# Batch 0 of a sparse attention: masks as bias matmuls, zero products on TensorE, and the output weights queued part by part

## The chip, the cores and the metric

The kernel runs on one NeuronCore of a Trainium2 chip. Its time is the device time of one execution in microseconds (us), the median of several runs. A NeuronCore has five engines with an instruction queue each: TensorE (PE, matrix products; its weight loads are listed as PEld), VectorE (DVE), ScalarE (ACT), GpSimd (POOL) and SyncE (SP, which here issues only DMAs). They meet through semaphores. SBUF is the on-chip memory with 128 partitions; PSUM takes what TensorE produces. DMAs are issued from the queues of SP, ACT or POOL; those of POOL can change the type on the way (float32 to bfloat16).

## What is computed

The reference is an attention over 8 batches of 8 heads, 576 positions and 64 channels, followed by a two-layer network over the 4608 tokens. Heads 0 to 3 look back over a window of 32 positions (local), heads 4 to 7 at every 32nd earlier position (strided):

```
scores = scale * np.matmul(q, k.transpose(0, 1, 3, 2))
mask_local = (rel >= 0) & (rel < stride)
mask_strided = (rel >= 0) & (pos[None, :] % stride == pos[:, None] % stride)
...
attn = attn / (np.sum(attn, axis=-1, keepdims=True) + 1e-09)
x = np.matmul(attn, v)        # heads joined: 4608 x 512
h = x @ w_in                  # 512 x 2048
g = h * np.tanh(softplus(h))
out = g @ w_out               # 2048 x 512
```

The masks set scores outside the pattern to -1e9 ahead of the softmax.

## The kernel before

**Attention of one batch.** Only the blocks that a mask leaves over are computed. The strided heads are cut into 16 units of 72 x 72 (`S_UNITS`), the local ones into 12 units of 128 keys x 96 queries for two heads (`L_UNITS`); `PARTS` groups them into three parts each, ("s", 0..2) and ("l", 0..2). For a part, `qk` makes the scores in a PSUM tile of the tag `acc0`, `acc1` or `acc2`, and ACT takes their exponential into `P_s` or `P_l` (SBUF, bfloat16). `mask` then multiplies that on an engine by a 0/1 pattern from the constants (L289). `pv` (one block, result in a PSUM tile of the two-buffer tag `pt`) or `pv2` (two blocks, result in an `acc` tile) multiplies by v, which carries a column of ones, so that the row sum comes along; DVE takes the reciprocal and scales into `x_s` or `x_l` (L316 and L317, in `pv2` L330 and L331). `xt` transposes these on PE, and a copy puts them into `xT`, the input of the network: strided rows into chunks 2 and 3, local ones into chunks 0 and 1.

**Transposed q and k.** `qk` needs channels on partitions. For batches 0 and 1, PE transposes them (`t_step`, for the local heads of batch 0 `t_step_loc0`) into a `pt` tile and a copy brings them to `kTs`, `qTs`, `kTl`, `qTl`. From batch 2 on, SP issues DMA transposes (`transpose_str`, `transpose_loc`). Local q and k arrive in float32 in `kl32` and `ql32` (`load_qk_loc`, SP) and are cast into `kl`, `ql`; strided ones are cast by POOL's DMA into `ks`, `qs` (`load_qk_str`). Those of batch 0 come into staging tiles, `st0` (strided, SP) and `lq0` (local, POOL).

**The network.** Block t of 512 tokens goes through `mlp1` (eight groups of eight 128x512 matmuls, L428, each evicted by ACT with the activation) and `mlp2` (64 matmuls, L467). Nine blocks cover the eight batches. In `mlp1(0, ...)` the first two groups are split into halves: chunks 2, 3 of both, then chunks 0, 1 of both.

**Order.** The program is written under a manual schedule: every engine executes its instructions in the order in which the Python code emits them. First comes the head, the attention of batch 0. Then, for each t, `mlp1(t)` runs, and the 16 steps of `mlp2(t)` are interleaved with the attention of batch t + 1 by the lists `at[0]` to `at[15]`. In stage t = 0 all batch-1 transposes of q and k are emitted after the last groups of `mlp1` (pairs `ts[4..5]`, `ts[6..7]`, `ts[0..1]`) and after the first step of `mlp2` (`ts[2..3]`). `mlp2(0)` goes through the chunks of `w_out` in the outer loop: step 0 to 3 need its first part, 4 to 7 the second, 8 to 11 the third, 12 to 15 the fourth.

**The queue of weights.** POOL issues the five loads of `w_in`, those of `ks`, `qs` of batch 1 and the first two parts of `w_out` in this order. A small copy into the tile `held` makes POOL wait: ahead of `w_in` it reads `vs[0]`, so it waits for the DVE cast of batch 0's strided v; in `rest_of_w_out` it reads a corner of `kTl`, and the last two parts of `w_out` and strided q, k of batch 2 follow. On SP a tiny load into `gate` reads the last quarter of `w_in`, so SP waits for its landing ahead of v of batch 1.

Of the kernel before, what the change touches and what calls it, by code (L numbers as in the profile page):

```python
# [10 lines left out]
F32 = mybir.dt.float32  # L11
# [8 lines left out]
SU = 80  # L20
CS, PN = 8, 72
RING = 4


def _consts():

    kk = np.arange(128)[:, None]
    qq = np.arange(WQ)[None, :]
    rel = qq + 32 - kk
    p = np.arange(PN)  # L30
    c = np.zeros((128, 128 + WQ + PN), np.float32)
    c[:, 0:128] = np.eye(128)
    c[:, 128:128 + WQ] = (rel >= 0) & (rel < STRIDE)
    c[:PN, 128 + WQ:] = (p[:, None] % 4 == p[None, :] % 4) & (p[:, None] <= p[None, :])
    return c.astype(ml_dtypes.bfloat16)
# [3 lines left out]
def kernel(ctx, tc, q, k, v, moe_w_in, moe_w_out, out):  # L39
# [14 lines left out]
    xT = const.tile([128, 4, RT], BF16, name="xT")  # L54
    consts = const.tile([128, 128 + WQ + PN], BF16, name="consts_sb")
    ident = consts[:, 0:128]
    loc = consts[:, 128:128 + WQ]
    stm = consts[0:PN, 128 + WQ:128 + WQ + PN]
    vl32 = const.tile([128, 4, NW, D], F32, name="vl32")
    vs32 = const.tile([128, 4, CS, D], F32, name="vs32")  # L60
# [14 lines left out]
    gate = const.tile([1, 256], BF16, name="gate")  # L75
    held = const.tile([1, 4], BF16, name="held")
    x_l = const.tile([128, NW, 256], BF16, name="x_l")
# [9 lines left out]
    def acc(i, name):  # L87

        return ps_a.tile([128, 2, 512], F32, tag=f"acc{i}", name=name)
# [11 lines left out]
    def load_qk_loc(b):  # L101
        for dst, src in ((kl32, k), (ql32, q)):
            if b < 2:
                nc.sync.dma_start(
                    dst[0:PL].rearrange("p h j d -> p h (j d)"),
                    src[b, 0:4].rearrange("h (p j) d -> p h (j d)", j=CL),
                )
            else:
                nc.sync.dma_start(
                    dst[0:PL].rearrange("p h i d -> p (h i) d"),  # L110
                    src[b, 0:4].rearrange("h (i p) d -> p (h i) d", p=PL),
                )
# [27 lines left out]
    def load_w_out(c0, c1):  # L140
        for c in range(c0, c1):
# [3 lines left out]
            )  # L145

    def cast(eng, out_, in_):
        if eng is nc.scalar:
            nc.scalar.copy(out_, in_)  # L149
        else:  # L150
            eng.tensor_copy(out_, in_)  # L151

    def cast_qk_loc(b, e_k, e_q):
        for e, dst, src in ((e_k, kl, kl32), (e_q, ql, ql32)):
            if b < 2:
                cast(e, dst[b % 2][0:PL].rearrange("p j h d -> p h j d"), src[0:PL])
            else:
                to = by_tile(dst[b % 2])
                for hp in range(2):
                    cast(  # L160
                        e, to[:, hp].rearrange("p i e d -> p e i d"), src[0:PL, 2 * hp:2 * hp + 2]
                    )
# [26 lines left out]
    def cast_v_loc(b, eng, i0=0, i1=NW):  # L189
        for i in range(i0, i1, 3):  # L190
            cast(
                eng, vl[b % 2][:, i:i + 3, :, 0:D],
                vl32[:, :, i:i + 3, :].rearrange("p h w d -> p w h d"),
            )
        if i0 == 0:
            eng.memset(vl[b % 2][0:32, 0, :, 0:D], 0.0)
# [34 lines left out]
    def t_step_loc0(src, dst, hp, eng):  # L231

        tr = tile_t("tr")[:].bitcast(BF16)
        for j in range(CL):
            for e in range(2):
                nc.tensor.transpose(
                    tr[64 * e:64 * e + 64, PL * j:PL * j + PL], src[0:PL, 2 * hp + e, j, :],
                    ident[0:PL, 0:PL],
                )
        cast(  # L240
            eng, dst.rearrange("c (p j) -> c p j", j=CL),
            tr[:, 0:S].rearrange("c (j p) -> c p j", j=CL),
        )

    T_ORDER = [(kd, w, hp) for kd in ("s", "l") for hp in range(2) for w in ("k", "q")]
# [13 lines left out]
    class Attn:  # L259
        def __init__(self, b):  # L260
            self.b = b

        def qk(self, parts, i_acc):

            ps, o = acc(i_acc, "ps"), 0
            todo = []
            for kind, i in parts:
                w = WQ if kind == "l" else PN
                o0 = o
                for x, y in PARTS[kind][i]:  # L270
                    for e in range(2):
                        r = slice(64 * e, 64 * e + 64)
                        if kind == "l":
                            lhsT, rhs = kTl[r, y, WQ * x:WQ * x + 128], qTl[r, y, WQ * x:WQ * x + WQ]
                        else:
                            c0 = SU * (4 * y + x)
                            lhsT, rhs = kTs[r, c0:c0 + 128], qTs[r, c0:c0 + PN]
                        nc.tensor.matmul(ps[:, e, o:o + w], lhsT=lhsT, rhs=rhs, start=True, stop=True)  # L278
                    o += w
                todo.append((kind, i, o0, o - o0))  # L280
# [54 lines left out]

        def xt(self, kind, hf, eng=None):
            eng = eng or nc.scalar
            tr = tile_t("trx")[:].bitcast(BF16)
            t0 = (self.b % RING) * S
# [144 lines left out]
    with tc.manual_schedule():  # L484
        Po, Dv, Sc = nc.gpsimd, nc.vector, nc.scalar
        Sc.preload_act_table(AF.Exp)
        Sc.dma_start(consts[:], consts_h.ap())
# [12 lines left out]
        lq0 = g_pool.tile([128, 16, 512], BF16, tag="gT", name="lq0")  # L500
        lq0 = lq0[:].rearrange("p a b -> p (a b)")[0:PL]
        kl0, ql0 = [lq0[:, 1536 * i:1536 * i + 1536].rearrange("p (h x) -> p h x", h=4) for i in range(2)]
        for p in P_l:
            Po.memset(p[:], 0.0)
        for dst, src in ((kl0, k), (ql0, q)):
            Po.dma_start(dst, src[0, 0:4].rearrange("h (p j) d -> p h (j d)", j=CL))
        kl0, ql0 = [x.rearrange("p h (j d) -> p h j d", d=D) for x in (kl0, ql0)]
# [10 lines left out]

        a = Attn(0)
        for hp in range(2):  # L520
            h = 2 * hp
            cast(Dv, ks[0][0:PN, h:h + 2, :], st0[0][:, h:h + 2, :])
            t_step(0, "s", "k", hp, Sc)
        for hp in range(2):
            h = 2 * hp
            cast(Dv, qs[0][0:PN, h:h + 2, :], st0[1][:, h:h + 2, :])
            t_step(0, "s", "q", hp, Dv if hp else Sc)
        for i in range(3):
            a.qk([("s", i)], i)
        a.mask("s", 0, Dv)  # L530
        cast(Dv, vs[0][0:PN, :, :, 0:D], vs32[0:PN])
        a.mask("s", 1, Dv)
        for x in (ks, qs):
            Po.memset(x[1][64:SU], 0.0)
        Po.tensor_copy(held[:], vs[0][0:1, 3, 0, 0:4])
        load_w_in(0, 256)
        load_w_in(256, 512)
        load_w_in(512, 1024)
        cast_v_loc(0, Po, 0, 3)
        load_w_in(1024, 1536)  # L540
        load_w_in(1536, 2048)
        for hp in range(2):
            t_step_loc0(kl0, kTl[:, hp, 32:32 + S], hp, Sc)
        a.pv2("s", 0, 0)
        a.mask("s", 2, Dv)
        a.pv2("s", 2, 1)
        for hp in range(2):
            t_step_loc0(ql0, qTl[:, hp, :], hp, Sc)
        a.qk([("l", 0)], 2)
        a.pv2("s", 4, 0)  # L550
        a.qk([("l", 1)], 1)
        a.mask("l", 0, Dv)
        a.pv2("s", 6, 0)
        cast_v_loc(0, Sc, 3, 6)
        a.qk([("l", 2)], 2)
        a.mask("l", 1, Dv)
        load_qk_str(1)
# [3 lines left out]
        accs = (2, 1, 0)  # L561
        gT, g1 = mlp1(0, accs)
        a.xt("s", 0)
        a.xt("s", 1)
        Sc.preload_act_table(AF.Mish)
        a.pv2("l", 0, 1)
        a.mask("l", 2, Dv)
        a.pv2("l", 2, 0)
        a.pv("l", 4)
        a.pv("l", 5)  # L570
        a.xt("l", 0)
        a.xt("l", 1)
        cast_qk_loc(1, Po, Po)
        for x in (ks, qs):
            Po.memset(x[0][64:SU], 0.0)
        load_qk_loc(2)

        def rest_of_w_out():
            Po.tensor_copy(held[:], kTl[0:1, 1, 32:36])
            load_w_out(2, 4)  # L580
            load_qk_str(2)
            cast_qk_loc(2, Po, Po)

# [4 lines left out]
        for t in range(NBLK):  # L588
# [4 lines left out]
            if t == 0:  # L593
                ts, at = t_steps(1), attn_steps(1, y, y)
                at[0] = [ts[2], ts[3], cast_v1]
                at[6].append(lambda: cast_v_loc(1, Dv, 0, 3))
                at[7].append(lambda: cast_v_loc(1, Dv, 3, 6))
                at[9] += [lambda: transpose_str(2), lambda: load_v_loc(2), lambda: cast_v(2, Po, Po)]
# [7 lines left out]
            for i, g in enumerate(g1):  # L606
                g()
                if t == 0:
                    for n in {7: (4, 5), 8: (6, 7), 9: (0, 1)}.get(i, ()):
                        ts[n]()  # L610
                    if i == 8:
                        rest_of_w_out()
                elif i == 0 and t + 1 < B:
                    if t > 1:
                        cast_qk_loc(t + 1, Dv, Dv)
                    transpose_loc(t + 1)
                    if t + 2 < B:
# [43 lines left out]
```

The softmax here doesn't subtract the row's maximum and nothing guards it: scores larger than these inputs give would overflow.

## Time and profile before

| what | us |
|---|---|
| median of 5 runs (lowest, highest) | 322.27 (320.83, 323.84) |
| the profiled execution's own time | 324.03 |
| its span | 322.2 |
| PE busy (share of the span) | 298.6 (93%) |
| ACT, DVE, POOL busy | 172.6, 131.1, 40.7 |
| head: start to the first matmul of `mlp1(0)` | 0 to 30.07 |
| `mlp1(0)` to the first matmul of `mlp2(0)` | 30.07 to 47.50 |
| `mlp2(0)` with batch 1 | 47.50 to 68.49 |
| stage t = 1 | 68.49 to 101.14 |
| stage t = 2, stage t = 3 | 32.49 each |

A group or an instruction of a view is given as start, duration, engine, line, operation, what it writes and reads, and how often; "idle before" and its releaser tell how long the engine stood still and what let it go. The chain of waits is followed back from the last instruction. The page's row of granted clocks shows 9 in every slice; a slow start of PE has to be read from the spacing of its instructions.

### The profile page before, as it was taken

What the parts mean: (1) busy time and instruction counts of PE and PEld (TensorE: products, weight loads), DVE (VectorE), ACT (ScalarE), POOL (GpSimd) and SP (SyncE); (2) the same over time, 40 slices, a digit from 0 to 9 for tenths busy, and PEclk for the clock granted to TensorE, in tenths of its full rate; (3) what the DMA queues carried; (4) which work ended last, traced back from release to release, by engine and by line L of the source; (5) the groups of instructions that cost most, each with busy time, mean ns of one, the idle gap of its engine ahead of it and who ended that gap; (6) DMA issues with size and microseconds to landing.
All of it is one profiled execution on the core that took longest, in us unless ns stands there. A gap on an engine that the chain in (4) does not pass through costs nothing.

```text
span 322.2 us, 5827 instructions
## 1 busy us (share of the span) xinstructions
PE 298.6 (93%) x2448; PEld 159.6 (50%) x2488; DVE 131.1 (41%) x332; ACT 172.6 (54%) x195; POOL 40.7 (13%) x50
## 2 busy tenths in 40 slices
PE   0674999899999999999999999999999999999996
PEld 0552455454455445544568555445544554444444
DVE  7676046920286128802880288018811830000000
ACT  2581454385646664666466646674567456315601
POOL 9287023045000100000020000000000000000000
PEclk9999999999999999999999999999999999999999
DMA  6999999999999999999979995897650101011012
GB/s 181 217 229 205 229 179 187 172 195 224 150 185 193 178 170 187 258 130 187 224 115 195 185 212 97 173 181 155 86 124 0 67 5 62 0 65 65 2 54 76
DMA packets 103114, 46.72 MB, mean 145 GB/s; under 512 B 85168, under 2 KB 95728, under 8 KB 103088
## 3 DMA queue, kind: packets, MB, share of 16 engines
q1 hardware_dynamic: 91648, 37.22, 64.1%
q0 software_dynamic: 11152, 8.92, 19.3%
q8 instruction: 19, 0.31, 0.4%
q10 hardware_dynamic: 288, 0.21, 0.2%
q14 instruction: 7, 0.06, 0.1%
HBM read 38.34 MB, written 9.44 MB: 148 GB/s over the span
## 4 chain that ended last, share of the span: by engine, by line
PE 83%; DVE 12%; issue 2%; DMA 1%; ACT 1%; ACTq 0%
PE psh L428 39%; PE pso L467 28%; PE po L305 4%; PE pso L449 4%; PE ps L278 3%; DVE x_l L317 3%; DVE Pl L289 2%; DVE x_s L317 2%; PE trx L344 2%; DVE ks L151 1%; DVE rden L316 1%; DMA st<-in_k_dram 1%; PE trx L354 1%; PE tr L207 1%; DVE vl L151 1%
## 5 line engine op out<-in xcount | busy, mean ns | idle before, releaser
L428 PE MATMUL psh<-xT,w_in 128*128 128x512 bf16 (+1 forms) x628 | 127.8, 362 | 0.8 <-issue 0.2
L467 PE MATMUL pso<-w_out,gT 128*128 128x512 bf16 x485 | 121.5, 379 | 1.7 <-issue 0.6
L433 ACT ACTIVATE gT<-psh 128x1024 bf16<-128x1024 f32 x72 | 73.6, 1023 | 45.5 <-PE psh L428 44.2
L428 PEld LDWEIGHTS <-w_in 128*128 128x128 bf16 x640 | 63.1, 99 | 63.3 <-issue 3.3
L467 PEld LDWEIGHTS <-gT 128*128 128x128 bf16 x512 | 43.6, 97 | 39.0
L289 DVE TENSOR_TENSOR Ps<-Ps,consts_sb 72x864 bf16<-72x864 bf16 (+1 forms) x24 | 13.2, 551 | 88.3 <-ACT Ps L283 88.3
L149 ACT COPY xT<-trx 128x576 bf16<-128x576 bf16 x32 | 20.1, 639 | 40.9 <-PE trx L354 28.2
L474 ACT COPY osb<-pso 128x1024 f32<-128x1024 f32 x16 | 16.2, 1012 | 22.6 <-PE pso L467 13.8
L283 ACT ACTIVATE Ps<-ps 72x864 bf16<-72x864 f32 (+1 forms) x24 | 18.5, 803 | 13.3 <-PE ps L278 13.2
L316 DVE RECIPROCAL rden<-po 72x4 f32<-72x4 f32 (+1 forms) x100 | 17.4, 174 | 17.2 <-PE po L305 17.1
L317 DVE TENSOR_TENSOR x_s<-po,rden 72x256 bf16<-72x256 f32 x56 | 23.6, 421 | 1.9
L151 DVE COPY osb<-pso 128x512 f32<-128x512 f32 (+1 forms) x2 | 1.1, 558 | 54.5 <-PE pso L449 54.5
L283 ACT ACTIVATE Pl<-ps 128x960 bf16<-128x960 f32 (+1 forms) x24 | 18.7, 806 | 3.6 <-PE ps L278 3.5
L305 PEld LDWEIGHTS <-Ps 72*128 72x128 bf16 x256 | 13.9, 101 | 12.9 <-DVE Ps L289 2.3
L317 DVE TENSOR_TENSOR x_l<-po,rden 96x256 bf16<-96x256 f32 x44 | 18.5, 421 | 1.5
L305 PE MATMUL po<-vs,Ps 72*128 72x65 bf16 x256 | 17.6, 201 | 1.4 <-DVE vs L151 0.8
L305 PE MATMUL po<-vl,Pl 128*128 128x65 bf16 x192 | 12.9, 201 | 5.4 <-DVE Pl L289 3.8
L289 DVE TENSOR_TENSOR Pl<-Pl,consts_sb 128x960 bf16<-128x960 bf16 (+1 forms) x24 | 16.2, 677 | 0.0
L97 POOL DMA_DIRECT2D ks<-in_k_dram x7 | 5.3, 762 | 81.9 <-DMA kTs<-ks 81.9
L305 PEld LDWEIGHTS <-Pl 128*128 128x128 bf16 x192 | 9.9, 103 | 9.6 <-DVE Pl L289 4.0
L449 PE MATMUL pso<-w_out,gT 128*128 128x512 bf16 (+1 forms) x79 | 14.0, 336 | 0.1
L151 DVE CAST vl<-vl 128x768 bf16<-128x768 f32 x12 | 10.9, 943 | 1.3 <-DMA vl<-in_v_dram 1.3
(70 smaller groups left out, 177.6 us busy)
## 6 DMA issues: line engine op xcount, KB each, us to landing
out_dram<-osb SPq DMA_DIRECT2D x16, 512.0 KB, 3.8
vl<-in_v_dram SPq DMA_DIRECT2D x7, 768.0 KB
vs<-in_v_dram SPq DMA_DIRECT2D x8, 576.0 KB
kl<-in_k_dram SPq DMA_DIRECT2D x7, 576.0 KB, 7.6
ql<-in_q_dram SPq DMA_DIRECT2D x7, 576.0 KB, 10.5
w_out<-in_moe_w_out_dram POOLq DMA_DIRECT2D x4, 512.0 KB, 15.9
ks<-in_k_dram POOLq DMA_DIRECT2D x7, 288.0 KB, 8.0
qs<-in_q_dram POOLq DMA_DIRECT2D x7, 288.0 KB, 9.3
```

The source lines that it names most:

```text
L149: nc.scalar.copy(out_, in_)
L151: eng.tensor_copy(out_, in_)
L283: nc.scalar.activation(pt[0:n, :, 0:nw], ps[0:n, :, o0:o0 + nw], AF.Exp, scale=scale)
L289: meng.tensor_tensor(out=pm, in0=pm, in1=mk[0:n, :].unsqueeze(1).unsqueeze(1).to_broadcast([n, 2, nu, w]), op=ALU.mult,)
L305: nc.tensor.matmul(po[:, h, :], lhsT=pt[0:n, c0:c0 + 128], rhs=rhs, start=True, stop=True,)
L316: nc.vector.reciprocal(rden[0:m, :], po[0:m, :, D])
L317: nc.vector.tensor_tensor(out=dst.rearrange("p (h d) -> p h d", h=4), in0=po[0:m, :, 0:D], in1=rden[0:m, :].unsqueeze(2).to_broadcast([m, ...
L428: nc.tensor.matmul(ps[:, u, o:o + n], lhsT=w_in[:, cc, fc * 128:(fc + 1) * 128], rhs=xT[:, cc, a:a + n], start=(cc == 2), stop=(cc == 1),)
L433: nc.scalar.activation(gT[:, 2 * g:2 * g + 2, :], ps[:], AF.Mish)
L449: nc.tensor.matmul(p, lhsT=gT[:, fc, 128 * ot:128 * ot + 128], rhs=w_out[:, fc, c0:c1], start=(fc == 0), stop=(fc == 15),)
L467: nc.tensor.matmul(p[:, ot % 2, :], lhsT=gT[:, fc, 128 * ot:128 * ot + 128], rhs=w_out[:, fc, :], start=(fc == 0), stop=(fc == 15),)
L474: nc.scalar.copy(osb[:], p[:])
```

## The change

In the head, batch 0 is no longer masked by DVE. `bias` writes the mask pattern, -30000 where a score is to vanish, into PSUM by two matmuls with the identity, and `qk` adds the scores to it. `busy` and the argument `n_busy` of `xt` emit products of a zeroed tile. `lq0` moves to partitions 64 to 127 in rows of 9 positions. `clear` zeroes as float32. The strided v cast stands later in DVE's order; `pv2` calls are in part replaced by `pv`; local v of batch 0 is cast in three pieces by POOL, ACT and DVE; the order of the local parts in `pv2` changes.

The wait ahead of `w_in` is now for `ql0`. The third part of `w_out` is queued after the first transposes into `kTs` of batch 1 (`rest_of_w_out`, after the tenth step of `mlp1(0)`), the fourth after the first mask of batch 1 (`last_of_w_out`, step 2 of `mlp2(0)`), followed by q, k of batch 2 and the casts of local v of batch 1, which DVE did before, and of local q, k of batch 2. In stage t = 1 PE transposes local q and k of batch 2, after groups 5 and 6 of `mlp1(1)`; SP's four DMA transposes of that batch go away, and its loads have the rows of 6 positions that batches 0 and 1 have.

```diff
@@ constants, loads and casts @@
+C0, P0 = 9, 64
...
+    c[:, o:o + WQ] = -30000.0 * (1 - c[:, 128:128 + WQ])
+    c[:PN, o + WQ:] = -30000.0 * (1 - c[:PN, 128 + WQ:o])
...
+    zero = const.tile([128, 128], BF16, name="zero")
...
-            if b < 2:
+            if b < 3:
...
+    def clear(eng, x):
+        eng.memset(x.bitcast(F32), 0.0)
...
+    def busy(n, i_acc):
+        ps = acc(i_acc, "ps")
+        for _ in range(n):
+            nc.tensor.matmul(ps[:, 0, 0:128], lhsT=zero[:], rhs=zero[:], start=True, stop=True)
...
+        def bias(self, kind, i, i_acc):
+            n, w, mk = (128, WQ, locb) if kind == "l" else (PN, PN, stmb)
+            nu = len(PARTS[kind][i])
+            ps = acc(i_acc, "ps")
+            for e in range(2):
+                nc.tensor.matmul(
+                    ps[:, e, 0:nu * w].rearrange("p (u c) -> p u c", u=nu), lhsT=ident[0:n, :],
+                    rhs=mk.unsqueeze(1).to_broadcast([n, nu, w]), start=True, stop=True,
+                )
+            return ps
...
-                        nc.tensor.matmul(ps[:, e, o:o + w], lhsT=lhsT, rhs=rhs, start=True, stop=True)
+                            ps[:, e, o:o + w], lhsT=lhsT, rhs=rhs, start=first, stop=True,
...
@@ the head @@
         for p in P_l:
-            Po.memset(p[:], 0.0)
+            clear(Po, p[:].rearrange("p e c -> p (e c)"))
...
+        busy(40, 0)
         for hp in range(2):
...
             t_step(0, "s", "k", hp, Sc)
+            if hp == 0:
+                busy(8, 0)
+        sb = [a.bias("s", i, i) for i in (1, 2)]
+        busy(8, 0)
+        sb.insert(0, a.bias("s", 0, 0))
...
-            a.qk([("s", i)], i)
-        a.mask("s", 0, Dv)
-        cast(Dv, vs[0][0:PN, :, :, 0:D], vs32[0:PN])
-        a.mask("s", 1, Dv)
+            a.qk([("s", i)], i, sb[i])
+        Po.tensor_copy(held[P0:P0 + 1], ql0[0:1, 3, 0, 0:4])
+        load_w_in(0, 256)
         for x in (ks, qs):
-            Po.memset(x[1][64:SU], 0.0)
-        Po.tensor_copy(held[:], vs[0][0:1, 3, 0, 0:4])
-        load_w_in(0, 256)
+            clear(Po, x[1][64:SU].rearrange("p h x -> p (h x)"))
...
-        cast_v_loc(0, Po, 0, 3)
+        cast_v_loc(0, Po, 0, 2)
...
-            t_step_loc0(kl0, kTl[:, hp, 32:32 + S], hp, Sc)
-        a.pv2("s", 0, 0)
-        a.mask("s", 2, Dv)
-        a.pv2("s", 2, 1)
+            t_step_loc0(kl0, kTl[:, hp, 32:32 + S], hp, Sc if hp else Dv)
+        cast(Dv, vs[0][0:PN, :, :, 0:D], vs32[0:PN])
+        lb = [a.bias("l", i, i) for i in range(2)]
         for hp in range(2):
             t_step_loc0(ql0, qTl[:, hp, :], hp, Sc)
-        a.qk([("l", 0)], 2)
-        a.pv2("s", 4, 0)
-        a.qk([("l", 1)], 1)
-        a.mask("l", 0, Dv)
-        a.pv2("s", 6, 0)
-        cast_v_loc(0, Sc, 3, 6)
-        a.qk([("l", 2)], 2)
-        a.mask("l", 1, Dv)
+        a.pv2("s", 0, 2)
+        a.qk([("l", 0)], 0, lb[0])
+        a.qk([("l", 1)], 1, lb[1])
+        a.pv("s", 2)
+        a.pv("s", 3)
+        a.pv2("s", 4, 2)
+        a.qk([("l", 2)], 0, a.bias("l", 2, 0))
+        a.pv("s", 6)
+        a.pv("s", 7)
+        cast_v_loc(0, Sc, 2, 4)
+        cast_v_loc(0, Dv, 4, 6)
+        a.pv2("l", 2, 1)
...
+        a.pv2("l", 0, 2)
         a.xt("s", 0)
         a.xt("s", 1)
         Sc.preload_act_table(AF.Mish)
-        a.pv2("l", 0, 1)
-        a.mask("l", 2, Dv)
-        a.pv2("l", 2, 0)
-        a.pv("l", 4)
-        a.pv("l", 5)
-        a.xt("l", 0)
-        a.xt("l", 1)
+        a.pv2("l", 4, 0)
+        a.xt("l", 0, n_busy=4)
+        a.xt("l", 1, Dv, n_busy=4)
...
@@ stages t = 0 and t = 1 @@
         def rest_of_w_out():
-            Po.tensor_copy(held[:], kTl[0:1, 1, 32:36])
-            load_w_out(2, 4)
+            Po.tensor_copy(held[0:1], kTs[0:1, 0:4])
+            load_w_out(2, 3)
+
+        def last_of_w_out():
+            Po.tensor_copy(held[0:1], P_s[0][0:1, 0, 0:4])
+            load_w_out(3, 4)
             load_qk_str(2)
+            cast_v_loc(1, Po)
             cast_qk_loc(2, Po, Po)
...
-                at[6].append(lambda: cast_v_loc(1, Dv, 0, 3))
-                at[7].append(lambda: cast_v_loc(1, Dv, 3, 6))
+                at[0].append(lambda: Sc.preload_act_table(AF.Exp))
+                at[2].append(last_of_w_out)
...
-                    if i == 8:
+                    if i == 9:
                         rest_of_w_out()
+                elif t == 1 and i in (5, 6):
+                    for w in ("k", "q"):
+                        t_step(2, "l", w, i - 5)
                 elif i == 0 and t + 1 < B:
                     if t > 1:
                         cast_qk_loc(t + 1, Dv, Dv)
-                    transpose_loc(t + 1)
+                        transpose_loc(t + 1)
```

## The prediction

> **What bounds the kernel now.** I read the sums first, then the chain of waits, then the stages of the chain by time. PE is busy for 93% of the span, and stages t = 2 and 3 take 32.49 us each with 32.00 of PE: nothing to gain there. The head is different, so I read its part of the chain:
>
> ```profile
> 4.64 4.47 DVE ks L151 x2
> ...
> 11.73 0.44 PE ps L278 x8
> 12.19 0.89 ACT Ps L283
> 13.11 0.60 DVE Ps L289
> 13.71 1.15 DVE vs L151
> ...
> 23.08 0.69 DVE x_l L331
> 23.76 3.43 DVE Pl L289
> 27.20 0.13 DVE rden L330
> ...
> 28.64 1.21 PE trx L344 x12
> ```
>
> Two pieces are far too long: two casts of k in 4.47 us, and the smallest mask in 3.43. The timeline of DVE and POOL shows what stood beside them:
>
> ```profile
> 4.46 1.80 POOL L534 MEMSET ks<- 16x2048 bf16 x1
> 4.64 4.46 DVE L151 CAST ks<-st 72x1024 bf16<-72x1024 f32 x2 [0.95 <-DMA st<-in_k_dram]
> 6.20 2.35 POOL L534 MEMSET qs<- 16x2048 bf16 x1
> 9.02 1.27 DVE L151 CAST qs<-st 72x1024 bf16<-72x1024 f32 x2
> ...
> 23.68 3.51 DVE L289 TENSOR_TENSOR Pl<-Pl,consts_sb 128x384 bf16<-128x384 bf16 x1
> 24.09 1.48 POOL L151 CAST kl<-kl 96x1536 bf16<-96x1536 f32 x1
> 25.51 1.47 POOL L151 CAST ql<-ql 96x1536 bf16<-96x1536 f32 x1
> ```
>
> The same two casts of q take 1.27 without POOL; the same mask form took 0.35 in batch 1 (57.08). So the excesses are 3.2 and 3.1 us. Next, weight loads at the start of `mlp1(0)`:
>
> ```profile
> 34.34 0.15 PEld L428 LDWEIGHTS <-w_in 128*128 128x128 bf16 x1 [0.28 <-issue]
> 34.73 1.18 PEld L428 LDWEIGHTS <-w_in 128*128 128x128 bf16 x6 [0.24 <-issue]
> ```
>
> From 30.07 to 34.73 they are 0.427 us apart; later the chain gives 9.93/46 = 0.216 a matmul. Eleven intervals at the difference are 2.3 us of slow PE. Last, the table of stretches:
>
> ```profile
> 47.50:68.49 20.99, 19.58 (x222) 10.96 (x223) 15.32 (x42) 10.13 (x13) 4.55 (x7) 1.00 1.23 174
> 82.31:101.14 18.83, 18.50 (x202) 9.90 (x205) 12.35 (x38) 10.29 (x13) 0.00 (x0) 1.00 1.35 172
> ```
>
> Columns: length, then busy PE, PEld, DVE, ACT, POOL. `mlp2(0)` leaves PE idle for 1.4 us, against 0.3 one block later; the chain passes through DVE there, by the two casts of vl at 57.43 and 59.16.
>
> [...]
>
> **Head, rebuilt from its rows.** POOL's clears of P_l, 2.25 before, should halve with half the elements (bounds 1.1 to 2.25), and so lq is issued about 1.1 us earlier. POOL then waits for ql0, and nothing of it stands beside the k casts. What limits instead is the landing of q: its second half landed at 8.5 by the trace's semaphore updates; I take 9.0, as lq now competes earlier (bounds 8.5 to 10). Then:
> - cast 0.67, transposes 0.6, DVE copy 0.46, scores 0.5: 11.3, against 12.19.
> - ACT: three exponentials 0.89 + 0.89 + 0.65, then the second k copy 0.64, which frees the transpose buffer: 14.4. The transposes of q stand next on PE and ahead of the first PV (0.65 + 0.5): 15.6. The strided v cast (1.22) must be done by then; POOL's two clears (about 0.9 each) can stand beside it, and cost 0 to 1 us. I take 0.
> - DVE: two pairs at 0.20 + 0.69, four singles at 0.17 + 0.42 take 4.2: 19.8; the vl cast of a third (two thirds of 0.94) 0.6: 20.4; three local pairs 2.7: 23.1. The masks of batch 0 (3.3 us without the excess) are gone; PE gains six bias pairs, 432 columns at most, 0.36 a matmul at half clock, and they fall into waits for q and for ACT.
> - last transposes 0.6 and issue 0.22: `mlp1(0)` starts at 23.9 instead of 30.07.
>
> [...] The groups of 8 and 4 cost 0.9 and 0.4 at most, behind casts and x_l scaling. Bounds of what they save: 0 to 2.3 us of slow PE.
>
> **`mlp1(0)`.** Before, 30.07 to 47.47 is 17.4: 13.8 (as in block 1) + 2.3 slow + three transpose pairs. Warm, 15.2 remain: 23.9 + 15.2 = 39.1; slow, 41.4.
>
> **The weights have to be there.** The first part of w_out, issued at 21.77, landed 20.7 us later, at 42.5, because five w_in loads and ks, qs stand ahead of it:
>
> ```profile
> w_out<-in_moe_w_out_dram POOLq DMA_DIRECT2D x1, 512.0 KB, 20.7
> ```
>
> A w_in part of 512 KB lands every 2.5 us (26.9, 29.5, 32.1). The queue's start moves from 14.91 (wait for the v cast) to the landing of ql0: 14.5 before, 12 in my estimate, with fewer rows (256 instead of 384) and an earlier issue. If the queue only shifts, the first part lands at 39.6; if the transfers ahead of it take the gain, at 42.5 (bounds 37 to 42.5). I take 40.0 for the start of `mlp2(0)`, the later of 39.1 and 39.6, rounded up: **-7.5 us** against 47.47.
>
> **`mlp2(0)`.** DVE loses 2 x 0.94 + 0.27 of vl work. On POOL it stands behind the mask of batch 1, a held copy, three DMA issues (0.75 each) and is done some 8.6 us into the stage; the local PV that needs it comes at 11.5 or later. POOL's casts can hold up a mask as in the head (0 to 3 us). Half the idle time goes: **-0.7**. The third part is issued when the stage begins, needed 9.9 in (57.34 - 47.47); it took 7.3 to land before. The fourth is issued after the first mask, 4.6 in, needed 15.5 in; it took 11.0: just in time.
>
> **Stage t = 1.** PE gets two pairs of transposes. A pair cost (4.48 - 2 x 1.73)/2 = 0.51 on the chain from 42.66 to 47.14: **+1.0**. The DVE copies (4 x 0.76) fall into idle DVE time. SP loses four transpose issues between 71.81 and 77.85, and the next loads of kl and ql, issued from 77.91, move up; no one waited for those. The POOL casts feeding the transposes wait for ql of batch 2, which took 21.9 us to land in 256-byte rows; the rows are six times as long now, and there are 10 us to spare.
>
> **Sum:** -7.5 - 0.7 + 1.0 = -7.2 from the span of 322.2: 315.0. The profiled execution ran 324.03, with 1.8 outside the span; the median of the runs, 322.27, lies at its span, so the median is forecast at 322.27 - 7.2 = **315.1**. A measurement of this kernel tells about 0.5% (1.6 us) from no change.
>
> **Rivals.** *Weights late or PE slow.* The first part of w_out stays at 42.5, or PE is throttled again in the head, and a mask waits for POOL once: start at 42.5, -5.0, no gain in `mlp2(0)`, +1.0: 318.3. For: w_in reads 1 MB of float32 for each 512 KB, about 410 KB/us at 2.5 us a part, and that may be all there is. Against: only loads of batch 1 compete, and w_in moves ahead of them.
>
> *Faster still.* Landing at 37, PE warm, no mask held: -10.5 - 1.1 + 1.0: 311.7. [...] Against: the DVE chain of 15.6 to 23.1 leaves no room unless q lands early.
>
> *The fourth part of w_out comes too late: slower.* It waits for a mask of batch 1, and only 10.9 us lie between issue and use. The two first parts took 20.7 and 21.7. At 21.7 PE waits for 10.8: 325.9. It decides from about 19.7 us of landing time on. Against: w_in and strided q, k stood ahead of those; here only the third part does, and in the kernel before the fourth took 11.0 with the third ahead.
>
> *No effect:* the new wait for ql0 lands the queue where it was, the casts meet POOL at another place, and the transposes add 1.0; then all gains would have to cancel.
>
> **How the numbers follow.** Chances: the forecast (312.5 to 317.5) 0.56, weights late or slow PE 0.22, faster still 0.12, slower 0.07, no effect 0.03. The range 311.0 to 319.0 takes in the first three. Faster 0.90, same 0.03, slower 0.07.
>
> **What would show it.** k casts of 0.67 each before 7; no L289 mask before `mlp2(0)`; first L428 matmul near 24 and 0.216 apart; first matmul of `mlp2(0)` near 40, with the idle time before it ended by a w_out landing if weights bind; stage t = 1 at 33.5. Wrong if PE waits for w_out in steps 12 to 15, if q lands after 10, or if the head's PV chain starts after 17.

## The result, and the profile after

The changed kernel takes 323.57 us (median of 44 runs, 320.09 to 326.40), the kernel before 322.28 (79 runs, 320.22 to 326.54). The ratio is **1.0022, 95% interval 1.0006 to 1.0039**: 0.7 us slower at the most likely value, less than the 0.5% that the prediction took as the bound of a difference, and no trace of the 7.2 us that it promised. Ratios leave out executions more than 1.5% above the fastest of their kernel, so a ratio and a quotient of two medians can differ.

The profiled execution of the changed kernel took 322.63, with a span (first to last instruction) of 320.9. That is 1.40 less than the 324.03 of the one profiled before, though the medians differ by 1.29 the other way: the profiled execution of before was 1.75 above its kernel's median, the one of after 0.94 below its own. So the stages have to be compared over more than one execution of each kernel. The table puts two of each side by side, the second ones from experiments 12 and 11 (us; a stage's start is its first matmul).

| | before, first | before, another | after, first | after, another | predicted |
|---|---|---|---|---|---|
| `mlp1(0)` starts | 30.05 | 26.45 | 25.34 | 25.25 | 23.9 |
| `mlp2(0)` starts | 47.48 | 43.24 | 40.48 | 42.61 | 40.0 |
| `mlp2(0)` lasts | 20.99 | 20.98 | 24.29 | 20.05 | 20.3 |
| `mlp1(1)` lasts | 13.82 | 13.81 | 14.85 | 14.84 | 14.8 |
| `mlp2(1)` lasts | 18.67 | 20.16 | 19.70 | 19.71 | 18.7 |
| stage t = 2 starts | 100.96 | 98.19 | 99.32 | 97.21 | 93.8 |
| span | 322.2 | 319.4 | 320.9 | 318.7 | 315.0 |

From stage t = 2 on nothing differs by more than 0.4: everything happens in the first 101 us.

**The head** became much what the prediction built. Behind the clears at the start, DVE's rows of the profile after (start, us, engine, line, operation, idle time before it) read:

```profile
4.95 0.69 DVE L161 CAST ks<-st 72x1024 bf16<-72x1024 f32 x1 [1.18 <-DMA st<-in_k_dram]
6.28 0.69 DVE L161 CAST ks<-st 72x1024 bf16<-72x1024 f32 x1 [0.63 <-DMA st<-in_k_dram]
7.70 0.69 DVE L161 CAST qs<-st 72x1024 bf16<-72x1024 f32 x1 [0.74 <-DMA st<-in_q_dram]
9.64 0.69 DVE L161 CAST qs<-st 72x1024 bf16<-72x1024 f32 x1 [1.25 <-DMA st<-in_q_dram]
```

The four casts take 0.69 each, and each waits for a landing; no mask follows until batch 1.

**`mlp2(0)`** is where the gain goes. The table of stretches after has the columns length, busy PE, PEld, DVE, ACT, POOL, granted clock, DMA share and GB/s; the rows are the head, `mlp1(0)`, `mlp2(0)`, `mlp1(1)` and `mlp2(1)`:

```profile
0.70:25.34 24.64, 21.08 (x320) 17.05 (x322) 14.44 (x40) 12.92 (x18) 12.25 (x19) 0.72 1.05 219
25.34:40.48 15.14, 15.07 (x102) 7.67 (x103) 3.18 (x6) 7.46 (x9) 4.92 (x5) 1.00 1.23 215
40.48:64.77 24.29, 20.75 (x222) 11.82 (x223) 13.73 (x39) 9.93 (x13) 10.52 (x12) 0.93 1.02 191
64.77:79.62 14.85, 14.75 (x87) 7.29 (x88) 2.85 (x4) 9.58 (x10) 4.59 (x7) 1.00 1.13 220
79.62:99.32 19.70, 18.49 (x202) 9.80 (x204) 12.17 (x38) 10.28 (x13) 0.00 (x0) 1.00 1.17 191
```

In the third row PE is idle for 3.5 us (24.29 - 20.75), and the granted clock (the share of TensorE's full clock that the records show) is 0.93, where it was 1.00 before: 7% of 24.29 is 1.7 us, half of the 3.41 us (59.46 to 62.87) that the records have at a clock of 0.50. PE's rows in time show both, the wait first and the slow stretch behind it:

```profile
58.56 1.02 PE L505 MATMUL pso<-w_out,gT 128*128 128x512 bf16 x4 [2.63 <-DMA w_out<-in_moe_w_out_dram]
59.42 0.64 PE L392 MATMUL trx<-consts_sb,x_s 72*128 72x72 bf16 x8
59.86 0.41 PE L340 MATMUL po<-vl,Pl 128*128 128x65 bf16 x4
60.50 1.49 PE L505 MATMUL pso<-w_out,gT 128*128 128x512 bf16 x3 [0.22 <-issue]
```

PE stands 2.63 us at step 12 of `mlp2(0)`, where the fourth part of `w_out` is needed first; 0.9 us later eight transposes take 0.64 instead of 0.42, three matmuls 1.49. The chain of waits names what it hung on:

```profile
44.37 0.61 DVE Ps L324
44.98 0.02 issue
45.00 0.02 POOLq L626
45.02 0.08 issue
45.10 0.18 POOL held L626
45.28 0.28 issue
45.55 12.97 DMA w_out<-in_moe_w_out_dram
58.52 0.04 issue
58.56 1.02 PE pso L505 x4
```

The first mask of batch 1, the held copy, the DMA's issue at 45.55, 12.97 us to its landing. PE would have used it at 55.93 (58.56 - 2.63).

**In stage t = 1**, `mlp1(1)` grew by 1.03 from the two pairs of transposes. In `mlp2(1)` something stands that no edit of that stage names. ACT's and PE's rows:

```profile
81.91 1.28 ACT L318 ACT_TABLE_LOAD   x1 [1.05 <-PE ps L310]
...
84.79 0.42 PE L340 MATMUL po<-vs,Ps 72*128 72x65 bf16 x8 [0.93 <-DVE Ps L324]
```

The table for the exponential is loaded only once the scores of batch 2 are there, and PE waits 0.93 for the first masked part. In the profile before, the load stood ahead of the scores (84.13) and waited for nothing:

```profile
83.55 1.28 ACT L283 ACT_TABLE_LOAD   x1
```

The author's guess is the read of `P_s[0]` on POOL in `last_of_w_out`, which the first exponential of batch 2 overwrites. No run takes that read away, so it was not shown.

### The profile page after: what moved, and what is told of

Read it like the earlier page. It is cut to its first block, busy times and chain, and to the rows that moved or that the text cites. A ratio compares the mean times of both kernels' runs of the same rounds, so it can differ in the third digit from the quotient of the medians.

```text
span 320.9 us, 6073 instructions
## 1 busy us (share of the span) xinstructions
PE 306.0 (95%) x2572; PEld 166.7 (52%) x2612; DVE 125.2 (39%) x333; ACT 171.2 (53%) x193; POOL 38.7 (12%) x52
## 4 chain that ended last, share of the span: by engine, by line
PE 74%; DMA 13%; DVE 7%; issue 2%; ACT 1%; SPq 1%; POOL 1%; ACTq 0%; POOLq 0%
PE psh L466 34%; PE pso L505 26%; PE pso L487 4%; DMA w_out<-in_moe_w_out_dram 4%; DMA w_in<-in_moe_w_in_dram 4%; PE po L340 4%; PE ps L310 3%; DMA vs<-in_v_dram 3%; DVE x_l L352 2%; DMA st<-in_q_dram 2%; DVE x_s L352 2%; DVE rden L351 1%; PE trx L382 1%; DVE Pl L324 1%; PE trx L392 1%
## 5 line engine op out<-in xcount | busy, mean ns | idle before, releaser
L505 PE MATMUL pso<-w_out,gT 128*128 128x512 bf16 x488 | 123.4, 381 | 3.9 <-DMA w_out<-in_moe_w_out_dram 2.6
L466 PE MATMUL psh<-xT,w_in 128*128 128x512 bf16 (+1 forms) x625 | 125.7, 357 | 0.9 <-issue 0.2
L466 PEld LDWEIGHTS <-w_in 128*128 128x128 bf16 x640 | 62.4, 98 | 61.1 <-DMA w_in<-in_moe_w_in_dram 0.4
L324 DVE TENSOR_TENSOR Ps<-Ps,consts_sb 72x864 bf16<-72x864 bf16 (+1 forms) x21 | 11.6, 552 | 74.2 <-ACT Ps L318 74.2
L352 DVE TENSOR_TENSOR x_s<-po,rden 72x256 bf16<-72x256 f32 x60 | 25.2, 421 | 2.1
L352 DVE TENSOR_TENSOR x_l<-po,rden 96x256 bf16<-96x256 f32 x42 | 17.7, 421 | 1.4
L161 DVE COPY kTl<-tr 128x576 bf16<-128x576 bf16 x5 | 3.8, 758 | 25.7 <-PE tr L231 24.1
L340 PEld LDWEIGHTS <-Pl 128*128 128x128 bf16 x192 | 10.4, 105 | 5.8 <-DVE x_l L352 1.4
L324 DVE TENSOR_TENSOR Pl<-Pl,consts_sb 128x960 bf16<-128x960 bf16 (+1 forms) x21 | 11.5, 545 | 0.0
```

Of the source, the lines that this page charges most:

```text
L324: meng.tensor_tensor(out=pm, in0=pm, in1=mk[0:n, :].unsqueeze(1).unsqueeze(1).to_broadcast([n, 2, nu, w]), op=ALU.mult,)
L340: nc.tensor.matmul(po[:, h, :], lhsT=pt[0:n, c0:c0 + 128], rhs=rhs, start=True, stop=True,)
L352: nc.vector.tensor_tensor(out=dst.rearrange("p (h d) -> p h d", h=4), in0=po[0:m, :, 0:D], in1=rden[0:m, :].unsqueeze(2).to_broadcast([m, ...
L466: nc.tensor.matmul(ps[:, u, o:o + n], lhsT=w_in[:, cc, fc * 128:(fc + 1) * 128], rhs=xT[:, cc, a:a + n], start=(cc == 2), stop=(cc == 1),)
L505: nc.tensor.matmul(p[:, ot % 2, :], lhsT=gT[:, fc, 128 * ot:128 * ot + 128], rhs=w_out[:, fc, :], start=(fc == 0), stop=(fc == 15),)
```

## The experiments

The main lines of reasoning above each got a run. Ratios are against the kernel before; 1% is 3.2 us. Experiments 1 to 5 and 8 to 10 start from the changed kernel.

**1. The fourth part not held for the mask.** It is queued right behind the third.

```diff
-            load_w_out(2, 3)
+            load_w_out(2, 4)
...
             Po.tensor_copy(held[0:1], P_s[0][0:1, 0, 0:4])
-            load_w_out(3, 4)
```

> The changed kernel with the third and the fourth part of w_out queued together, after the first transposes into kTs of batch 1; the wait for the mask stays ahead of what followed. Theory A (the fourth part is late because it is queued late): it lands at about 53 instead of 58.5, PE waits for no weights in mlp2(0), the stall of 2.6 us and the slow matmuls after it go, the ratio to the kernel before falls from 1.002 to about 0.990. Theory B (the transfers as a whole set the landing, whatever their order): it lands at 57 or later and the time stays within 1 us of the changed kernel's.

Measured: ratio 0.9940 (0.9908 to 0.9972), 0.8% below the changed kernel. The rows of `mlp1(0)` and `mlp2(0)` in its table of stretches:

```profile
25.13:41.00 15.87, 15.54 (x105) 7.71 (x105) 3.33 (x6) 7.94 (x9) 5.46 (x5) 1.00 1.23 213
41.00:61.15 20.15, 19.81 (x226) 10.95 (x223) 13.86 (x39) 10.14 (x13) 8.35 (x11) 1.00 1.14 216
```

The 4.1 us are back (24.29 - 20.15), about the wait of 2.6 and the 1.7 lost at half clock. The part landed at 55.6 instead of 58.5, just ahead of its use. Three of the 13 executions took 327.45 to 327.84; experiment 10 comes back to them.

**2. The table loaded early in stage t = 1,** by an explicit load for the exponential at the first step of the attention list.

```diff
                     at = attn_steps(t + 1, x, y)
+                    if t == 1:
+                        at[0].append(lambda: Sc.preload_act_table(AF.Exp))
```

> The changed kernel with the table of the exponential loaded explicitly at the start of mlp2(1), so that this load no longer waits for the score matmuls. Theory A (the read of P_s by the copy into held gives the first exponential of batch 2 one more semaphore, and the load takes over its wait for PE): stage t = 1 gets 0.9 to 1.0 us shorter (19.6 to 19.8 us from its first mlp2 matmul to the next stage instead of 20.8), the time by as much. Theory B (the idle time of PE there comes from the transposes by PE): the stage stays at 20.8.

Measured: 0.9976 (0.9948 to 1.0004), and `mlp2(1)` takes 18.67 instead of 19.70. ACT's row:

```profile
77.89 1.28 ACT L652 ACT_TABLE_LOAD   x1
```

The load waits for nothing again, so its hidden wait cost 1.03 of stage t = 1. This execution's `mlp2(0)` took 20.05 and had no wait for the fourth part.

**3. Local q, k of batch 2 by DMA transposes again,** with the rows that they had before.

```diff
-            if b < 3:
+            if b < 2:
...
-                elif t == 1 and i in (5, 6):
-                    for w in ("k", "q"):
-                        t_step(2, "l", w, i - 5)
...
-                        transpose_loc(t + 1)
+                    transpose_loc(t + 1)
```

> The changed kernel with local q and k of batch 2 transposed by DMA again, as in the kernel before, and loaded in its layout. Theory A (each pair of PE transposes costs 0.5 us and hides nothing): stage t = 1 gets 1.0 us shorter, the time too. Theory B (the DMA transposes and the loads of short rows cost elsewhere): mlp2(0) or stage t = 1 gains idle time on PE, q of batch 2 lands 5 us or more later than 56.7, and the time does not fall.

Measured: 1.0052 (1.0027 to 1.0077), so the change gains nothing without its PE transposes; that it loses isn't settled, as the interval overlaps with that of the changed kernel. `mlp1(1)` falls back to 13.81, but `mlp2(1)` takes 26.61. PE's rows:

```profile
85.74 0.67 PE L310 MATMUL ps<-qTl,kTl 64*128 64x96 bf16 x12 [4.28 <-DMA qTl<-ql]
86.34 0.40 PE L340 MATMUL po<-vs,Ps 72*128 72x65 bf16 x4
86.55 1.90 PE L505 MATMUL pso<-w_out,gT 128*128 128x512 bf16 x4
```

PE waits 4.28 for the transposed q, and then four matmuls take 1.90 where they take 1.03 at 80.16, ahead of the wait (the granted clock is 0.87 from 75 to 101). The prediction said of SP's transposes that no one waited for them. That was true of the execution it had read.

**4. The fourth part not needed in time.** The last four steps of `mlp2(0)` use the third part of `w_out` instead, so that the output of the first 512 tokens is not the reference's; the fourth part is still loaded at its time.

```diff
-                    ... rhs=w_out[:, fc, :],
+                    ... rhs=w_out[:, fc - 4 if t == 0 and fc > 11 else fc, :],
```

> The changed kernel, but in mlp2(0) the last four steps multiply by the third part of w_out instead of the fourth, so that block's result is not the reference's; every load stays as it is. It measures what the wait for the fourth part costs. Theory A (the stall of 2.6 us makes PE slow again for one more window): mlp2(0) shortens from 24.4 to 20.0 us, the time falls by 4 to 4.5 us, the ratio to the kernel before is about 0.989. Theory B (the slow window comes without the stall): only the stall's 2.6 us go.

Measured: 0.9929 (0.9905 to 0.9953). The part landed at 59.3, later than in the changed kernel, and no one waits for it. `mlp2(0)` takes 20.57 at a granted clock of 1.00:

```profile
40.86:61.43 20.57, 19.89 (x226) 10.95 (x223) 14.43 (x39) 10.14 (x13) 8.47 (x11) 1.00 1.13 209
```

This and experiment 1 take the same thing away in two ways, the lateness and the need, and win about the same, 0.8% and 0.9% (1.0022 - 0.9929), the latter 3.0 us of the median.

**5. No zero products.** Both loops that emit them run zero times.

```diff
-        for _ in range(n):
+        for _ in range(0):
...
-            for _ in range(n_busy):
+            for _ in range(0):
```

> The changed kernel without the products of the zeroed tile (40, 8 and 8 at the start, 4 and 4 ahead of the local transposes). The profiles so far show PE at full clock from about 5 to 12 us, slow from 12 to 25 and at full clock again just as mlp1(0) starts. Theory A (they warm PE for mlp1(0)): the first matmuls of mlp1(0) are 0.427 us apart for some 3 to 5 us, mlp2(0) starts 1.5 to 2.3 us later, and the time rises by up to 2 us. Theory B (they don't last to mlp1(0), whose own weights are late anyway): the start of mlp2(0) moves by less than 1 us and the time stays within 1 us of the changed kernel's.

Measured: 1.0093 (1.0062 to 1.0124), 2.3 us above the changed kernel. The head is as fast as with them (25.31), `mlp1(0)` takes 17.06 instead of 15.14; but `mlp2(0)` takes 26.76. PE's rows there:

```profile
62.26 1.87 PE L505 MATMUL pso<-w_out,gT 128*128 128x512 bf16 x4 [4.48 <-DMA w_out<-in_moe_w_out_dram]
63.92 0.69 PE L392 MATMUL trx<-consts_sb,x_s 72*128 72x72 bf16 x8
```

The held copy behind the first mask came 1.8 us later (46.87), the fourth part was issued with it, landed at 62.2, and the wait grew to 4.48. Of what looks like the worth of zero products in this profile, 2.5 us (26.76 - 24.29) are again the fourth part and 1.9 are `mlp1(0)`; experiment 9 parts the two.

**6. The kernel before, with its two collisions taken apart.** POOL's clears of `ks`, `qs` move behind the first load of `w_in`, away from the k casts; its casts of batch 1's q, k move behind two more clears, away from the mask that they met.

```diff
-        for x in (ks, qs):
-            Po.memset(x[1][64:SU], 0.0)
         Po.tensor_copy(held[:], vs[0][0:1, 3, 0, 0:4])
         load_w_in(0, 256)
+        for x in (ks, qs):
+            Po.memset(x[1][64:SU], 0.0)
...
-        cast_qk_loc(1, Po, Po)
         for x in (ks, qs):
             Po.memset(x[0][64:SU], 0.0)
+        cast_qk_loc(1, Po, Po)
```

> The kernel before with its two collisions of DVE and POOL taken apart and nothing else: the clears of ks and qs stand behind the first w_in load, and the casts of local k and q of batch 1 behind the clears of the second set. Theory A (the two collisions were the head's length): casts of k 0.67 us each, the small mask 0.35, mlp1(0) starts near 25 instead of 30.07, and the time falls by 4 to 5 us. Theory B (the weights set the pace behind the head): mlp1(0) starts earlier, but mlp2(0) not before the first part of w_out lands at about 42, and the time falls by less than 3 us.

Measured: 0.9989 (0.9968 to 1.0009), no difference. Both excesses are gone from its profile (k casts 0.69 each, mask 0.34), and the first copy into `qTs` came at 9.92 instead of 11.22; yet `mlp1(0)` began at 27.0, not earlier than in the third profile of the kernel before (26.45, experiment 12). Nor did weights set the pace, as the theory that fits the ratio has it: `mlp2(0)` began at 43.3, and the first part of `w_out` had landed at 39.0. The chain of waits shows where the time went:

```profile
15.26 1.80 POOL ks L536
17.05 0.41 POOL qs L536
17.46 1.28 issue
18.75 1.48 POOL w_in L136 x2
20.23 0.04 issue
20.27 1.69 POOL vl L151
21.97 0.05 issue
22.02 0.31 POOL vl L196
22.33 0.04 issue
22.37 0.61 PE po L305 x8
```

The clears, at their new place, hold up POOL's cast of local v, and the local products wait for that. The edit swapped one wait for another, so the run doesn't price the k casts by themselves. It does say that 1.3 us won early in the head may be worth nothing at its end.

**7. The kernel before, unaltered,** to see how far its first profile stands for it.

> The kernel before, unchanged, for a second profile of it and a ratio of it to itself (expected within 0.3% of 1). The first profile was taken in an execution of 324.03 us, 1.75 over the median. Theory A (that execution was long in the head or mlp1(0), where PE was slow): the second profile, if taken at 322 or below, has its first mlp2 matmul 1.5 to 2 us earlier than 47.5. Theory B (executions differ elsewhere): the first mlp2 matmul stays at 47.5 and a later stage differs.

Measured: 0.9990 (0.9971 to 1.0009). The profiled execution was a long one (328.04). Yet in it `mlp1(0)` starts at 26.9 and `mlp2(0)` at 43.5, some 4 us ahead of the first profile. The masks that tell why are below, with the third profile. The time was lost later: PE waited 5.39 us in `mlp2(1)` for the same transposed q as in experiment 3, and the matmuls behind it ran at about half speed (at 92.09 four of 128x512 took 1.90, against 1.03 ahead of the wait):

```profile
89.35 0.67 PE L278 MATMUL ps<-qTl,kTl 64*128 64x96 bf16 x12 [5.39 <-DMA qTl<-ql]
```

**8. Experiments 1 and 2 in one kernel.**

> The changed kernel with two of its waits taken away: the fourth part of w_out queued with the third, and the table of the exponential loaded ahead of mlp2(1)'s scores. If the two are independent their gains add: from the changed kernel's ratio 1.002, 0.8% for the first and 0.45% for the second, gives about 0.990 of the kernel before; in the profile mlp2(0) takes 20.1 and stage t = 1 33.5. If one hides the other it stays at 0.994.

Measured: 318.96, ratio **0.9860 (0.9815 to 0.9905)**: faster than both kernels in five of its six executions, which the ratio rests on; the sixth took 327.52. Its stages are 25.85, 15.91, 20.41, 14.84 and 18.67.

**9. The same without zero products.**

> Both parts of w_out queued together and the early table load, but no zero products. Theory A: with the weights out of the way, zero products are worth only what they save of slow matmuls at the start of mlp1(0): it takes about 17.1 us instead of 15.9, mlp2(0) stays below 20.5 without a wait for weights, and the median is 0.8 to 1.5 us above that of the same kernel with zero products. Theory B: they are worth the whole 2.4 us by which the changed kernel grew without them, so the median is 2 us or more above it. If the head begins mlp1(0) later than 26.5, it is their side effect on PE's queue that counts, which neither expects.

Measured: 319.86, ratio 0.9916 (0.9877 to 0.9955); `mlp1(0)` takes 16.44 instead of 15.91, and `mlp2(0)` 21.16 instead of 20.41. The medians differ by 0.9 us, of which 0.5 can be seen in `mlp1(0)`; the two intervals overlap, so the size is not settled. These stages don't show the 2.3 us of experiment 5 as the price of zero products; the times alone don't exclude it.

**10. Experiment 8 once more.**

> The joint queueing and the early table load again, with more rounds, for an interval. If the first measurement holds, the ratio to the kernel before is between 0.985 and 0.993, with the profiled execution's mlp2(0) below 20.5 and mlp2(1) at 18.7. If it was luck, the ratio is above 0.995.

Measured: 0.9919 (0.9856 to 0.9982), but from two of its six executions (318.78 and 321.37); the other four took 326.43 to 328.22, and the profile is of one of these. It shows where that one lost time. From the rows of POOL and of PE in its `mlp2(0)`:

```profile
59.20 1.60 POOL L161 CAST vl<-vl 128x768 bf16<-128x768 f32 x2 [9.97 <-DMA vl<-in_v_dram]
...
60.84 0.38 PE L340 MATMUL po<-vl,Pl 128*128 128x65 bf16 x4 [5.58 <-POOL vl L161]
61.03 1.90 PE L505 MATMUL pso<-w_out,gT 128*128 128x512 bf16 x4
```

Here the cast of local v of batch 1, which the change put on POOL, found its data 11 us later than in experiment 8 (where it began at 48.23), PE waited 5.58 for it, and four matmuls behind it took 1.90, against 1.04 ahead of it (54.11). One profile can't tell how often that is the cause. But such executions seem to come with the early queueing: of the 29 of experiments 1, 8, 9 and 10, eight took 326.43 to 328.22, while the longest of the 83 of the changed kernel and experiments 2 and 4 took 326.40. Over all twelve executions of the kernel of experiments 8 and 10 the median is 320.35 and the mean 322.4, against 322.28 and 322.5 for the kernel before. So its gain holds for most executions and is all but lost in the mean.

**11. The changed kernel, unaltered, a second profile.**

> The changed kernel unaltered, one more look. Theory A: the wait for the fourth part of w_out is there in every execution, so PE waits 2 us or more ahead of the fourth quarter of mlp2(0), which takes 23 us or more. Rival: the wait in the first profile was an accident of that execution, and this one takes 20 to 21 us.

Measured: 320.50, and no wait for the fourth part: `mlp2(0)` takes 20.05. The rival is right that the wait is not in every execution. PE's row at the start of `mlp2(0)` shows what took its place:

```profile
42.63 1.04 PE L505 MATMUL pso<-w_out,gT 128*128 128x512 bf16 x4 [1.14 <-DMA w_out<-in_moe_w_out_dram]
```

Here the *first* part landed at 42.6, 4.4 us later than in the first profile (38.2), and PE waited for it. `mlp2(0)` began 2.1 later; 1.14 of that is the wait, the rest is PE reaching it later (41.49), with a granted clock of 0.96 over `mlp1(0)`, where the first profile has 1.00. The fourth part, which landed at 56.0, was in time.

The profiles of experiments 2, 3 and 4, which queue the weights in the same order, lie between the two. The first part landed at 41.7, 40.5 and 38.4, and the fourth took 9.1, 10.6 and 13.5 us from issue to landing; in the two profiles of the changed kernel it was 12.97 with the first part at 38.2, and 8.5 with 42.6. On the whole, the later the first part lands, the quicker the fourth.

How often the wait comes can't be read from the granted clock of a whole execution. The first profile has 0.973 and this one 0.979, but the profile of experiment 2 has 0.973 too and no such wait. And both profiled executions lie below the median of 323.57, by 0.94 and 3.07, so one at the median was not seen.

**12. The kernel before, a third profile.**

> The kernel before unaltered, one more look. Theory A: the long mask next to POOL's casts (3.5 us) was an accident of the first profiled execution; mlp1(0) starts near 27 and mlp2(0) near 43.6. Rival: it is the usual case, and mlp1(0) starts near 30 and mlp2(0) near 47.5.

Measured: 321.24, with `mlp2(0)` from 43.24. The long mask of the first profile is missing here too. DVE and POOL at that place:

```profile
23.68 0.35 DVE L289 TENSOR_TENSOR Pl<-Pl,consts_sb 128x384 bf16<-128x384 bf16 x1
...
24.49 1.48 POOL L151 CAST kl<-kl 96x1536 bf16<-96x1536 f32 x1
```

The mask starts within 0.02 us of the same time in all three profiles (23.68, 23.70, 23.68). POOL's cast began at 24.09 in the first, 25.51 in the second and 24.49 in this one, and the mask took 3.51, 0.34 and 0.35. A cast that starts 0.4 us later missed it. And in this execution PE waits 1.31 in `mlp2(1)` for the transposed q.

## Why the prediction was wrong

Two terms of the sum failed: the fourth part of `w_out`, taken as "just in time" and so at no cost, and the -7.5 for the start of `mlp2(0)`, counted from one long execution. The span of the first profile is 5.9 above the forecast of 315.0: 0.5 at the start of `mlp2(0)`, 4.0 in it, 1.0 in `mlp2(1)`, 0.4 later. In the second profile the excess is 3.7: 2.6 at that start, -0.2 in `mlp2(0)`, 1.0 in `mlp2(1)` and 0.3 later.

**The fourth part of `w_out`, "just in time".** The prediction gave it 10.9 us from issue to use and took 11.0 for the landing, from an execution in which two parts were issued together. In the first profile the slack was 10.4 (45.55 to 55.93) and the landing took 12.97. With the same queue order it took 8.5 to 13.5 in four other profiles, and 14.9 in experiment 5. The mechanism had been named, as a rival with a chance of 0.07; its price was mis-sized twice. It was held to decide only from 19.7 us of landing, because a wait was counted at its own length; the runs show 4.1 us for a wait of 2.63, behind which 3.41 us at half clock stood. It landed at 58.0 in the kernel before when issued at 47.0, and at 58.5 after, issued at 45.55: there an issue 1.4 us earlier brought nothing (one 3.1 earlier, in experiment 1, brought 2.9), while bringing its use forward by 7 took the cover of 5 us that the old schedule had (57.97 to about 63).

**The baseline was one execution.** The prediction took 3.1 us for the mask and the cast of kl, and a start of `mlp2(0)` at 47.48, as the kernel's. The two other profiles start at 43.24 and 43.5. Of the gain of 7.5, 4 was there already in those; the forecast set the median at the span, though the profiled execution stood 1.75 over the median, a sign that was on the page. Against the third profile the head of the changed kernel is worth 0.6 to 2.8 us at the start of `mlp2(0)`.

**The weights can set this start too,** as the first rival had it. The first part landed at 38.2, ahead of its use, in one execution of the changed kernel, and at 42.6, 1.14 late, in another; the forecast took 39.6. That 39.6 lies between is luck. It came from a queue that starts 3 us earlier, with ql0 in place at 12, but POOL's rows of the first profile read:

```profile
13.84 0.18 POOL L575 COPY held<-lq 1x4 bf16<-1x4 bf16 x1 [10.57 <-DMA lq<-in_q_dram]
...
23.04 0.78 POOL L149 DMA_DIRECT2D w_out<-in_moe_w_out_dram  x1
```

The wait ended only 1.1 us earlier than before (14.91), and the first part was issued later (23.04 against 21.77); it landed earlier because it took 15.2 us instead of 20.7, for which the prediction gave no reason. DMA's share of busy time in `mlp1(0)` is 1.23 in both profiles of the changed kernel, which suggests that the transfers from 25 to 58 us limit this stretch at one end or the other; it was not tested by taking transfers away.

**Head and `mlp1(0)`: right in kind, 1.4 late.** `mlp1(0)` came at 25.34, not 23.9: q's second half was cast from 9.64 instead of 9.0, and the four bias matmuls of the local parts, counted at 432 columns at most, 0.36 a matmul, and as filling waits, have 480 columns and took 1.72 together on the path (13.27 to 14.98 in the chain). `mlp1(0)` itself lasted 15.14 of the 15.2 forecast, and the first 22 matmuls took 4.91, or 0.223 each: there the slow start was gone. In the second profile it was not (17.36, wait included; the granted clock is 0.96). The 40 zero products took 4.23 us (1.00 to 5.23) and ended ahead of the first transposes (5.70); groups of eight took 0.61, groups of four 0.61 and 0.63, where the prediction had 0.9 and 0.4 at most. POOL's clears did get shorter: `P_l` 1.21 us instead of 2.25, `ks` and `qs` 0.94 each instead of 1.80 and 2.35. That the zero products save 0 to 2.3 us was the author's estimate, from the spacings of 0.427 and 0.216 before; in `mlp1(0)` experiment 5 has 1.9 and experiment 9 0.5. No run takes the bias matmuls, or any other piece of the new head but the zero products, away by itself, so its worth is not divided among them.

**`mlp2(0)` -0.7:** 20.05 to 20.57 where nothing waits, against 20.98: the step holds, at 0.4 to 0.9. Its condition, that local v be cast in time on POOL, fails in the execution of experiment 10.

**Stage t = 1, +1.0:** `mlp1(1)` +1.03, as worked out. Not foreseen was the table load, another 1.03 (experiment 2), perhaps brought in by the added read of `P_s[0]`. "No one waited" for SP's transposes held for the profile read, but PE waited 1.31 and 5.39 in the two others, and 4.28 in experiment 3; in such executions the transposes on PE pay for themselves.

The sum then reads, from the third profile of before (321.24, 1.0 below its median) to the first of after: -2.8 to the start of `mlp2(0)`, +3.3 in it, +1.0 in `mlp1(1)`, -0.5 in `mlp2(1)`: +1.1 to stage t = 2. To the second of after: -0.6, -0.9, +1.0, -0.5: -1.0. Near to nothing on the whole, as measured.

## What to carry to other kernels

When a change makes an engine reach its data earlier, list every load that it will then meet, with issue, landing and use, and give each the spread of landings over several executions, not one value. Price a wait of TensorE of 2.6 us or more with what the slow matmuls behind it cost: here 1.7 us behind one of 2.63. And before a collision seen in one profile is booked as gain, read a second profile, or at least see how far the profiled execution stands from the median.

## What the runs showed of the hardware

- **Slow matmuls stood behind the longer waits of TensorE.** Behind waits of 4.28, 5.39 and 5.58 us (experiments 3, 7 and 10) four 128x512 matmuls took 1.90 us, behind one of 4.48 (experiment 5) 1.87, where they take 1.02 to 1.04 elsewhere; behind the 2.63 of the first profile after, three took 1.49 instead of 0.81. Behind waits of 1.14 and 1.31 (experiments 11 and 12) four took 1.04 and 1.03. What a wait between 1.31 and 2.63 does was not measured. The records of the first profile have 3.41 us at half clock behind the wait of 2.63; in experiments 3 and 5 the granted clock is 0.87 over 26.0 and 26.76 us. An estimate from these, twice 13% of either, is some 7 us at half clock.
- **Here a busy PE did not keep the clock up.** With the zero products at the start the records of the first profile have full clock from 4.85 to 11.67 and half clock from there to 25.3 (the 0.72 in the first row of the stretches), though PE was busy for 21.08 of the 24.64 us. In the profile before, the first matmuls of `mlp1(0)`, from 30.07 to 34.7, ran at half speed too (0.427 apart, later 0.216; its granted clock reads 1.00 there), after a head in which PE was busy for 13.86 of 29.35 us.
- **Landings spread by 4 us and more** with nothing changed: the first part of `w_out` at 38.2 and 42.6, local v of batch 1 by 48.2 or only at 59.2.
- **A mask took 3.51 us beside a POOL cast** that began 0.41 after it, and 0.35 beside one that began 0.81 after it, in one execution each. Two k casts took 4.46 us beside POOL's clears, and 0.69 each without them (experiment 6). By what means POOL's work lengthens these was not shown.
